# An mLSTM cell followed by a tanh-shrink MLP: ranks of a list schedule from due times, scores of the first two units ahead of their gates, shorter fillers, and a last output in four blocks

## The chip, the core and the metric

The kernel runs on one core of one Trainium2 chip. The metric is the device time of one execution, in microseconds (us), as the median of several runs. Below, PE is the TensorE engine, DVE is VectorE, ACT is ScalarE, POOL is GpSimd and SP is SyncE; PEld is PE's loading of weights, which overlaps its matmuls.

## The reference

Everything is float32. A recurrent cell with a matrix as its state runs over time for each batch and head; its output is reshaped to 3072 tokens of 320 features and goes through two matrix products with `h - tanh(h)` between them.

```python
batch, n_heads, seq, head_dim = (4, 8, 768, 40)
for t in range(S):
    m_new = np.maximum(f_gate[:, :, t] + m, i_gate[:, :, t])
    f_stab = np.exp(f_gate[:, :, t] + m - m_new)
    i_stab = np.exp(i_gate[:, :, t] - m_new)
    m = m_new
    C = f_stab[:, :, None, None] * C + i_stab[:, :, None, None] * np.einsum('bhd,bhe->bhde', vt, kt)
    n = f_stab[:, :, None] * n + i_stab[:, :, None] * kt
    h_tilde = np.einsum('bhde,bhe->bhd', C, qt)
    denom = np.maximum(np.abs(np.einsum('bhd,bhd->bh', n, qt)[:, :, None]), 1.0)
    y[:, :, t] = h_tilde / (1.0 + np.exp(-o_gate[:, :, t])) / denom
# bridge: (B,H,S,D) -> (B*S, H*D)
x = np.ascontiguousarray(y.transpose(0, 2, 1, 3)).reshape(B * S, H * D)
# MLP: n_tokens, d_model, d_ff = (3072, 320, 2048)
h = x @ w_in
g = h - np.tanh(h)
out = (g @ w_out).astype(np.float32)
```

## The kernel before

**Units of the cell.** The recurrence is done in chunks of 128 time steps, in closed form. A *unit* is one batch element with all 8 heads in one chunk: 4 batches x 6 chunks are 24 units, numbered chunk by chunk, so units 0 to 3 are the first chunk. For each unit the kernel makes the scores `ps` (PE, from the loaded `kz` and `qz`), a causal mask of them in `P` (DVE; for the units in `BY_POOL` ACT copies and POOL selects), the values scaled by gate factors in `vs` (DVE, with one more column from ACT), the sum over the chunk in `ph` (PE), the division by the denominator and the output gate (`den`, `o`, `ys`: DVE and ACT; the division by shares of heads on ACT is called "shares"), the update of the state (`pc` on PE, the decay of `state`), and the transposes of `ys` to `xT` (`px` on PE), which is the input of the MLP. Units of later chunks go through DRAM for the transpose (`zt` to `h_rows` to `z_in`, `yt` to `y_rows` to `xT`). The gate factors of a chunk are made from the loaded gates by two transposes and two products on PE (`gate`), with rows of DVE and ACT work between.

**The MLP.** Two units make a *group* of 256 tokens: 12 groups. The 2048 hidden features are 8 pairs of 128-feature blocks. An *item* is one group with one or a few pairs: `ph_up` (PE, h), the squares and polynomials of `g` (`z`, `q`, `gt` on ACT and DVE), and the product with `w_out` (`po`). Groups 0 and 1 run in plain form while the weights still arrive, in the nine items 0 to 8 of `RUNS`. From `START`, item 9, on, groups 2 to 11 use seven products in place of eight for each 2 x 2 block of blocks (products `ph_up<-xT,sums_in` and `pS`, with sums of weights `sums_in` and differences of weights `wT` made once, and sums `s` of `gt`). Here ACT carries partial sums from bank to bank (`ph_up<-ph_up`). This is the *long stage*.

**The weights** come in as pieces of a 64-bit format and are put together on the chip: POOL issues the fetch into a buffer `w`, ACT makes two parts (`w_e`, `w_r`), DVE shifts one, an adder makes `w_m`, and DVE sets the sign into `w_in` or `w_out`. The string `ADDERS` says for each of the 16 blocks whether the adder is POOL (G) or DVE (V). There are four buffers `w`; a fetch waits for the `sign` step of the block four earlier.

**What sets the order.** The program is written out by a list scheduler, the class `Plan` (L135). Each operation is added with an engine, a modelled duration, the operations that it needs, the buffers (tokens) that it takes and gives, and a rank. `run` (L214) picks, over and over, the ready operation with the earliest modelled start, and by rank where starts tie; an operation with a positive rank is charged `WAIT` = 0.2188 us of start. Its choice is then fixed: `Pinned` and `T.keep` chain each engine's instructions in that order, so on the chip an engine never overtakes its own queue. The table `BY` says which engine does which kind of step. `plan_gates`, `plan_unit`, `plan_weights`, `plan_plain`, `plan_down`, `plan_seven` and `plan_late` add the operations.

**Fillers.** Where the model sees PE idle before the long stage, `idle` and `stream` (L445) put in matmuls of a constant tile `lit` into a bank that nobody reads (`awake<-lit`, 128x512). They compute nothing. Their number is fixed when the program is written; the chip runs them whether PE would have waited or not.

**The end.** `last_parts` adds the last group's banks of products together into `ob` on DVE in three steps and stores each from SP; the register load `load_count` prepares a branch to a fallback that the runs here don't take.

Of the kernel before, what the change touches and what calls it, by code (L numbers as in the profile page):

```python
# [60 lines left out]
L = 128  # L61
# [18 lines left out]
def kernel(  # L80
# [54 lines left out]
    class Plan:  # L135
# [8 lines left out]
        AGE = -0.4021  # L144
# [10 lines left out]
        def add(self, engine, us, step, after=(), rank=0.0, take=(), give=(), at=0.0, kb=0.0, tiles=1, hold=0.0, dense=1.0, lag=None, small=False, port=False, late=False):  # L155
# [3 lines left out]
                  "lag": self.LAG[engine] if lag is None else lag, "small": small, "port": port and engine in "VG", "late": late}  # L159
# [53 lines left out]

        def run(self, idle, fill):  # L214
            for op in self.todo:
                op["then"] = []
# [151 lines left out]
    G.memset(k_tiles[:, :, H:], 0.0)  # L368
    G.memset(vs_tiles[:, :, H * D1:], 0.0)
# [35 lines left out]
    load_unit(0, ("qz",), A)  # L405
    load_gates(0, 1)
# [10 lines left out]
    load_unit(1, ("qz",), A)  # L417
# [18 lines left out]
    load_unit(0, ("v",), G)  # L436
# [546 lines left out]
    def down_seven(some):  # L983
# [4 lines left out]
        def product(where, a, x, b):  # L988
# [4 lines left out]
            if first:  # L993
                pool, tag = ((ps_o, "po0"), (ps_o, "po1"), third[g])[bank]
                tag = tag if isinstance(tag, str) else tag["small"]
                pS[g][bank] = pool.tile([128, 2 if bank else 3, HM], FP, name=f"pS{bank}", tag=tag)
# [5 lines left out]
        for k in (0, 1, 5, 3, 4, 2, 6) if final else range(7):  # L1002
            for x, (_, p) in enumerate(some):
# [3 lines left out]
                    ((0, 2), a11, even[:, 0]), ((0, 0), a12, odd[:, 0]), ((2, 1), a22, wT[p][:, 3]),  # L1007
# [34 lines left out]
    def last_parts(g):  # L1042
# [11 lines left out]
        def store(x, n=1):  # L1054
            at = [out[row_of(g * GT + y // 2):, y % 2 * HM:].offset for y in (x, x + n - 1)]
            blocks = [[at[1] - at[0], n]] if n > 1 else []
            SP.dma_start(out=bass.AP(out.tensor, at[0], [[DM, L], *blocks, [1, HM]]), in_=ob[:, x:x + n] if n > 1 else ob[:, x])

        def first():
            A.copy(out=a, in_=bank[0][:, 2])  # L1060
            V.tensor_tensor(out=ob[:, 0:5:4], in0=bank[0][:, 0:2], in1=twice(a), op=OP.add)
            store(0)

        def second():
            V.tensor_tensor(out=u, in0=bank[1], in1=twice(ob[:, 4]), op=OP.add)
            V.tensor_tensor(out=ob[:, 3], in0=bank[1][:, 0], in1=u[:, 1], op=OP.add)
            store(3)
# [251 lines left out]
    RANKS = (-1.0, -1.0, 15.2966, -19.6693)  # L1319
    WEIGHTS = (0.08, -3.8727, 8.9593, 4.7376, 13.1429, 47.5005, 2.7491, 9.7033)  # L1320
    START = item(FIRST * NP)
    LATER_GATES = (13.4508, 52.4651)
    SECOND_GATES = (7.6004, 15.8868)
    HOLD = 16.8771
    FETCH = {(0, 1): 6.5462, (2, 1): -9.4480, (3, 0): 9.5391, (3, 1): 34.7367}
    APART = ()
# [60 lines left out]
    LATE = {"o": -4.9124, "k": -11.0257, "q2": -0.0286, "v": 0.9346}  # L1387

    def plan_unit(n, rank):
# [10 lines left out]
        if n < 2:  # L1400
            u["qz"] = plan.add("N", 0.0, lambda: arrive(n), at=(6.4, 7.8)[n] - 1.7)
            if n == 0:
                u["v"] = plan.add("N", 0.0, lambda: None, at=7.0 - 1.7)
            else:
                u["v"] = plan.add("G", 0.6, lambda: [load_unit(n, ("v",), G), arrive(n)], at=5.5, rank=-1.0, kb=164)
# [10 lines left out]
        def first_part():  # L1416
# [4 lines left out]
            for step in ready[0]:  # L1421
# [594 lines left out]
```

## Time and profile before

| what | value |
|---|---|
| three runs, us | 511.04, 505.89, 509.83 |
| median, us | 509.83 |
| profiled execution, us | 506.61 |
| its span, us | 504.9 |
| mean granted PE clock | 0.996 |
| bytes moved | 52.39 MB, 104 GB/s over the span |
| first product in seven (start of the long stage) | 127.72 us |
| last matmul ends | 498.08 us |

The span runs from the first to the last instruction of the profiled execution; its own time also holds what lies around the span, 1.7 us. All instants and durations of the trace belong to that execution, which is 3.2 us shorter than the median of the three runs.

### The profile page before, as it was taken

What the parts mean: (1) busy time and instruction counts of PE and PEld (TensorE: products, weight loads), DVE (VectorE), ACT (ScalarE), POOL (GpSimd) and SP (SyncE); (2) the same over time, 40 slices, a digit from 0 to 9 for tenths busy, and PEclk for the clock granted to TensorE, in tenths of its full rate; (3) what the DMA queues carried; (4) which work ended last, traced back from release to release, by engine and by line L of the source; (5) the groups of instructions that cost most, each with busy time, mean ns of one, the idle gap of its engine ahead of it and who ended that gap; (6) DMA issues with size and microseconds to landing.
All of it is one profiled execution on the core that took longest, in us unless ns stands there. A gap on an engine that the chain in (4) does not pass through costs nothing.

```text
span 504.9 us, 14174 instructions
## 1 busy us (share of the span) xinstructions
PE 494.6 (98%) x5376; PEld 433.5 (86%) x5376; DVE 381.9 (76%) x928; ACT 298.4 (59%) x832; POOL 174.7 (35%) x294
## 2 busy tenths in 40 slices
PE   8999999999999999999999999999999999999994
PEld 4775776777799999999999999999999999899984
DVE  3779989656578778788788788788788788685853
ACT  3465675365467567557567567557567666654540
POOL 4698987686542143041243043042022020000000
PEclk9999999999999999999999999999999999999998
DMA  7964675353543643542643553553443452310001
GB/s 225 285 207 128 205 190 147 61 99 88 117 100 81 127 101 77 112 110 68 132 110 84 109 113 87 107 111 85 93 103 86 89 107 44 71 31 0 27 1 32
DMA packets 138217, 52.39 MB, mean 104 GB/s; under 512 B 116512, under 2 KB 129504, under 8 KB 138144
## 3 DMA queue, kind: packets, MB, share of 16 engines
q1 hardware_dynamic: 126888, 27.50, 26.9%
q0 software_dynamic: 8032, 20.00, 14.2%
q10 hardware_dynamic: 3224, 3.93, 2.3%
q8 instruction: 44, 0.72, 0.6%
q14 instruction: 29, 0.24, 0.2%
HBM read 38.94 MB, written 12.45 MB: 102 GB/s over the span
## 4 chain that ended last, share of the span: by engine, by line
PE 89%; DVE 6%; issue 2%; POOL 1%; ACT 0%; DMA 0%; SPq 0%; DVEq 0%; ACTq 0%
PE ph_up L129 38%; PE pS L129 30%; PE po L129 6%; PE pT L129 5%; PE ps L129 3%; PE awake L129 3%; DVE gt L106 2%; PE pc L129 2%; POOL w_m L106 1%; PE ph L129 1%; DVE w_e L106 1%; DVE sums_in L106 0%; DMA z_in<-h_rows 0%; PE gate L129 0%; DVE w_out L106 0%
## 5 line engine op out<-in xcount | busy, mean ns | idle before, releaser
L129 PE MATMUL ph_up<-xT,w_in 64*64 64x256 f32 (+3 forms) x1316 | 156.5, 349 | 0.0
L129 PEld LDWEIGHTS ph_up<-xT,w_in 128*128 128x128 f32 (+2 forms) x1316 | 114.6, 162 | 18.5 <-issue 5.2
L106 POOL TENSOR_TENSOR ys<-z_in,o 128x256 f32<-128x256 f32 (+1 forms) x40 | 22.9, 583 | 239.2 <-ACT o L106 229.3
L129 PE MATMUL ph_up<-xT,sums_in 128*128 128x128 f32 x624 | 95.5, 276 | 0.7 <-issue 0.5
L106 ACT ACTIVATE z<-ph_up 128x256 f32<-128x256 f32 (+1 forms) x98 | 40.7, 417 | 87.5 <-PE ph_up L129 87.2
L129 PEld LDWEIGHTS ph_up<-xT,sums_in 128*128 128x128 f32 x624 | 84.9, 191 | 2.4 <-ACT ph_up L106 0.8
L129 PE MATMUL pS<-wT,s 128*128 128x160 f32 x480 | 81.4, 300 | 0.0
L106 DVE TENSOR_TENSOR both<-ph_up,cs 128x256 f32<-128x256 f32 x78 | 32.9, 422 | 62.7 <-PE ph_up L129 60.2
L106 DVE SCALAR_TENSOR_TENSOR gt<-q,gt 128x512 f32<-128x512 f32 (+1 forms) x98 | 71.3, 735 | 7.4 <-ACT q L106 1.0
L106 ACT COPY ph_up<-ph_up 128x256 f32<-128x256 f32 x117 | 41.8, 357 | 57.5 <-PE ph_up L129 48.8
L106 ACT ACTIVATE q<-z,tiny 128x512 f32<-128x512 f32 (+1 forms) x98 | 69.9, 713 | 1.9
L129 PEld LDWEIGHTS pS<-wT,s 128*128 128x128 f32 x480 | 69.0, 190 | 0.4 <-issue 0.4
L106 ACT ACTIVATE o<-o,den 128x40 f32<-128x40 f32 x168 | 56.4, 411 | 5.9 <-DVE den L106 5.9
L129 PE MATMUL pS<-w_out,gt 128*128 128x160 f32 x320 | 56.6, 311 | 0.0
L129 PEld LDWEIGHTS pS<-w_out,gt 128*128 128x128 f32 x320 | 45.1, 190 | 4.4 <-issue 2.3
L106 DVE SCALAR_TENSOR_TENSOR gt<-ph_up,z 128x256 f32<-128x256 f32 (+1 forms) x98 | 41.4, 457 | 6.0 <-ACT z L106 6.0
L106 POOL DMA_DIRECT2D v<-in_v x62 | 37.5, 609 | 2.0 <-issue 2.0
L129 PE MATMUL po<-w_out,gt 128*128 128x320 f32 x128 | 37.7, 440 | 0.2 <-DVE gt L106 0.2
L129 PEld LDWEIGHTS po<-w_out,gt 128*128 128x128 f32 x128 | 23.3, 190 | 9.6 <-DVE gt L106 0.9
L106 DVE TENSOR_TENSOR s<-gt 128x256 f32<-128x256 f32 x80 | 30.6, 405 | 0.3
L129 PE MATMUL pS<-wT,gt 128*128 128x160 f32 x160 | 29.9, 300 | 0.0
L129 PE MATMUL pS<-w_out,s 128*128 128x160 f32 x160 | 28.9, 300 | 0.1
(122 smaller groups left out, 728.0 us busy)
## 6 DMA issues: line engine op xcount, KB each, us to landing
w<-in_moe_w_out POOLq DMA_DIRECT2D x8, 640.0 KB, 5.1
h_rows<-zt SPq DMA_DIRECT2D x80, 64.0 KB
z_in<-h_rows SPq DMA_DIRECT2D x80, 64.0 KB
w<-in_moe_w_in POOLq DMA_DIRECT2D x16, 256.0 KB, 4.1
kz<-in_kT SPq DMA_DIRECT2D x48, 80.0 KB
qz<-in_qT SPq DMA_DIRECT2D x44, 80.0 KB
o<-in_o_gate POOLq DMA_DIRECT2D x20, 160.0 KB, 2.6
y_rows<-yt SPq DMA_DIRECT2D x80, 40.0 KB
```

The lines of the kernel that those rows point to most:

```text
L106: i = method(*args, **kwargs)
L129: return cls.keep(nc.tensor.matmul(*args, **kwargs))
```

## The change

The work stays the same but for the fillers; what moves is where each instruction stands in its engine's queue, and for some which engine it is on.

1. *Ranks from due times.* Operations of the long run of items get a due time (`due`), and a pass backward through the plan hands it to what they need, less durations. Off PE an operation's rank is now this due time plus `BLEND` = 0.1443 of its old rank. About forty rank constants have new values.
2. *Scores first.* For units 0 and 1 the scores are issued in two halves ahead of the gates' PE work; unit 1's go into the two banks of `ph_up` (`APART`). The loads of unit 1's `qz` (ACT's queue) and unit 0's `v` (POOL's queue) move to the head, two memsets on POOL behind them.
3. *Other engines.* `ADDERS` has another pattern, the decay of `state` goes from DVE to POOL, and the differences `wT` that are made late from POOL to DVE.
4. *Fillers* can be a quarter to a whole of 512 columns long, and `idle` counts them in quarters up to 14 us.
5. *The last output* is made and stored in four blocks in place of three, the last one in two halves of 64 rows from SP and ACT; `load_count` comes behind it.

```diff
+        BLEND = 0.1443
         def run(self, idle, fill):
+            for op in reversed(self.todo):
+                for a in op["after"]:
+                    a["due"] = min(a["due"], op["due"] - a["us"] - (0.0 if a["engine"] == op["engine"] == "T" else a["lag"]))
+            for op in self.todo:
+                if op["engine"] != "T":
+                    op["rank"] = op["due"] + self.BLEND * op["rank"]
...
-    ADDERS = "GGGGGVGGGGVGVGVV"
+    ADDERS = "VGGGVVGGGGVGVGVV"
-    BY = {"prep": "V", "share": "A", "product": "G", "decay": "V", "sum_in": "G", "sum_out": "V", "late_out": "G", "kz": "S", "qz": "S", "v": "G", "k": "G", "o": "G", "out": "S", "in": "S", "y": "S", "x": "S"}
+    BY = {"prep": "V", "share": "A", "product": "G", "decay": "G", "sum_in": "G", "sum_out": "V", "late_out": "V", "kz": "S", "qz": "S", "v": "G", "k": "G", "o": "G", "out": "S", "in": "S", "y": "S", "x": "S"}
...
     load_unit(0, ("qz",), A)
+    load_unit(1, ("qz",), A)
+    load_unit(0, ("v",), G)
     load_gates(0, 1)
...
     def stream(bank, n):
-        for _ in range(n):
-            T.matmul(bank.rearrange("p (h t) -> p h t", h=HH), lit, lit.unsqueeze(1).to_broadcast([128, HH, L]), start=True, stop=True)
+        for first in range(0, n, HH):
+            k = min(HH, n - first)
+            T.matmul(bank.rearrange("p (h t) -> p h t", h=HH)[:, 0:k], lit, lit.unsqueeze(1).to_broadcast([128, k, L]), start=True, stop=True)
...
         def first():
             A.copy(out=a, in_=bank[0][:, 2])
             V.tensor_tensor(out=ob[:, 0:5:4], in0=bank[0][:, 0:2], in1=twice(a), op=OP.add)
-            store(0)
+            store(0, SP)
...
         def third():
-            V.tensor_tensor(out=ob[:, 1:3], in0=bank[2], in1=u, op=OP.add)
-            store(1, 2)
-        in_parts.extend((second, first, third))
+            V.tensor_tensor(out=ob[:, 2], in0=bank[3][:, 0], in1=u[:, 1], op=OP.add)
+            store(2, A)
+        def fourth():
+            V.tensor_tensor(out=ob[:, 1], in0=bank[2][:, 0], in1=u[:, 0], op=OP.add)
+            store(1, SP, A)
+        in_parts.extend((first, second, third, fourth))
...
-    RANKS = (-1.0, -1.0, 15.2966, -19.6693)
+    RANKS = (-1.0, -1.0, 18.2675, -24.8287)
-    APART = ()
+    APART = (1,)
...
+        if n < 2:
+            names = ("up0", "up1") if n in APART else ("a",)
+            op = plan.add("T", 0.5, first_part, [u["qz"]], rank, [(name, held) for name in (*names, "P")], tiles=2, dense=0.6)
+            u["scores"] = plan.add("T", 0.5, other_part, [op], rank, tiles=2, dense=0.6)
...
+    DUE0, DUE1 = 19.0, 4.7354
+    def when(x):
+        return DUE0 + DUE1 * (sum(map(len, items[:x])) + 2 * max(0, x - len(items)))
...
-            if final and k == 5 and ends:
-                downs.append(plan.add("T", 0.1, load_count, [op], rank))
+            if final and k == 6 and ends:
+                downs.append(plan.add("T", 0.1, load_count, [op, e], rank))
...
-        one = 0.43 if t0 < plan.COLD[0] else 0.217
+        one = 0.108 if t0 < WARM else 0.217
```

Three places in the queues follow. Each row is an instruction or a run of equal ones (x8), with its line, its operation, the tile that it writes and the tiles that it reads.

The first place is PE's queue at the start of the program: the scores `ps` of units 0 and 1, the gates' transposes and products `gate`, and the fillers `awake` around them. Before, the scores of unit 0 stand behind the gates:

```order
L129 LDWEIGHTS lit
L129 MATMUL awake<-lit 128x512
L133 MATMUL gate<-ident,sums_in 128x32
L133 MATMUL gate<-ident,xT_90 128x32
L129 MATMUL gate<-lfT,upto 128x32
L129 MATMUL gate<-lfT,ones 120x32
L129 MATMUL ps<-qz,kz 128x128 x8
L129 LDWEIGHTS lit
L129 MATMUL awake<-lit 128x512
```

And now:

```order
L129 LDWEIGHTS lit
L129 MATMUL awake<-lit 128x128
L129 MATMUL ps<-qz,kz 128x128 x16
L133 MATMUL gate<-ident,sums_in 128x32
L133 MATMUL gate<-ident,xT_90 128x32
L129 LDWEIGHTS lit
L129 MATMUL awake<-lit 128x512
L129 MATMUL gate<-lfT,upto 128x32
L129 MATMUL gate<-lfT,ones 120x32
```

Both units' scores (x16) have moved ahead of the gates' first transpose, and one filler stands between the transposes and the products. Ahead of these rows stood 9 full fillers before and stand 7 and a quarter now.

The second place is PE's queue around the `ph` of the first chunk's last units, with items of the MLP (`ph_up`, `po`) between. Before:

```order
L129 MATMUL ph<-vs,P 128x41 x8
L129 MATMUL ph_up<-xT_87,w_in 128x256 x2
L129 MATMUL ps<-qz,kz 64x2x64 x4
L129 MATMUL ps<-qz,kz 64x64 x4
L129 MATMUL ps<-qz,kz 64x2x64 x4
L129 MATMUL ps<-qz,kz 64x64 x4
L129 MATMUL gate<-ei,ident 64x32 x2
L129 MATMUL po<-w_out,gt 128x320 x4
L133 MATMUL px<-ident,ys_144 128x128 x3
```

Behind these rows 25 full fillers follow, and then the `ph` of unit 3. Now:

```order
L129 MATMUL ph_up<-xT_87,w_in 128x256 x2
L129 MATMUL ph<-vs,P 128x41 x8
L129 MATMUL ph_up<-xT_87,w_in 128x256 x4
L129 MATMUL po<-w_out,gt 128x320 x2
L133 MATMUL px<-ident,ys_146 128x128 x3
L129 MATMUL pc<-vs,k 64x41 x8
L129 MATMUL po<-w_out,gt 128x320 x2
L133 MATMUL px<-ident,ys_145 128x128 x3
L133 MATMUL gate<-ident,sums_in 128x32
```

Between the two `ph` of the last units now stand two fillers and two products of `ph_up`, and no run of fillers is left at this place.

The third place is POOL's queue at about the fourth block of weights: the fetches of blocks (`DMA`), the adds `w_m`, and the two selects of unit 2's masks in `P`. Before:

```order
L106 DMA w_345<-in_moe_w_in 128x256 x2
L106 DMA w_345<-in_moe_w_in 64x128 x2
L106 TENSOR_TENSOR w_m<-w_e,w_r 128x640
L106 AFFINE_SELECT P<-P 128x512
L106 TENSOR_TENSOR w_m<-w_e,w_r 128x640
L106 AFFINE_SELECT P<-P 128x512
```

And now:

```order
L106 DMA w_319<-in_moe_w_in 128x256 x2
L106 DMA w_319<-in_moe_w_in 64x128 x2
L106 TENSOR_TENSOR w_m<-w_e,w_r 128x640
L106 TENSOR_TENSOR sums_in<-w_in 128x2x128
L106 TENSOR_TENSOR sums_in<-w_in,sums_in 128x128
L106 DMA w_388<-in_moe_w_out 128x2x320
L106 TENSOR_TENSOR w_m<-w_e,w_r 128x640
L106 AFFINE_SELECT P<-P 128x512 x2
```

The two selects stood apart behind one add each; now both stand behind two adds, two sums and another fetch. Over the whole program the count of full fillers on PE goes from 94 to 29, with 5 of half and 1 of a quarter length beside them; POOL's adds go from 11 to 9 and DVE's from 5 to 7; 32 differences `wT` move from POOL to DVE and 16 decays from DVE to POOL.

More of the change, by code (lines that the diff above doesn't have):

```diff
@@ L153, in __init__, with add @@
             self.port = {"V": 0.0, "G": 0.0}
-        def add(self, engine, us, step, after=(), rank=0.0, take=(), give=(), at=0.0, kb=0.0, tiles=1, hold=0.0, dense=1.0, lag=None, small=False, port=False, late=False):
+        def add(self, engine, us, step, after=(), rank=0.0, take=(), give=(), at=0.0, kb=0.0, tiles=1, hold=0.0, dense=1.0, lag=None, small=False, port=False, late=False, due=1000.0):
             self.serial += 1
@@ L1052, in twice, with store @@
             return t.unsqueeze(1).to_broadcast([128, 2, HM])
[L1054 to L1057, printed above, removed]
+        def store(x, *queues):
+            at = out[row_of(g * GT + x // 2):, x % 2 * HM:].offset
+            rows = L // len(queues)
+            for i, queue in enumerate(queues):
+                queue.dma_start(out=bass.AP(out.tensor, at + i * rows * DM, [[DM, rows], [1, HM]]), in_=ob[i * rows:(i + 1) * rows, x])
         def first():
@@ L1425, in plan_unit @@
         bank = "a"
-        u["scores"] = plan.add("T", 1.0, first_part, [u["qz"], *(of(n - 2, "second") if n in (2, 3) else [])], rank, [(bank, held), ("P", held)], tiles=2, hold=HOLD * (n // B), dense=0.4 if n else 0.6)
-        if n in BY_POOL:
+        if n < 2:
+            names = ("up0", "up1") if n in APART else ("a",)
+            op = plan.add("T", 0.5, first_part, [u["qz"]], rank, [(name, held) for name in (*names, "P")], tiles=2, dense=0.6)
+            u["scores"] = plan.add("T", 0.5, other_part, [op], rank, tiles=2, dense=0.6)
+            u["mask"] = [plan.add("V", 0.62, lambda i=i: ready[1][i](), [u["scores"]], rank - 7.2169, give=[(names[i], held)] if n in APART else [(names[0], held)] if i else ())
+                         for i in range(2)]
+        else:
+            u["scores"] = plan.add("T", 1.0, first_part, [u["qz"], *(of(n - 2, "second") if n in (2, 3) else [])], rank, [(bank, held), ("P", held)], tiles=2, hold=HOLD * (n // B), dense=0.4 if n else 0.6)
+        if n < 2:
+            pass
+        elif n in BY_POOL:
             copies = [plan.add("A", 0.55, lambda i=i: ready[1][i][0](), [u["scores"]], rank - -2.0678, give=[(bank, held)] if i else ()) for i in range(2)]
@@ L1430, in plan_unit @@
         else:
-            u["mask"] = [plan.add("V", 0.62, lambda i=i: ready[1][i](), [u["scores"]], rank - 10.5159, give=[(bank, held)] if i else ())
+            u["mask"] = [plan.add("V", 0.62, lambda i=i: ready[1][i](), [u["scores"]], rank - 6.0391, give=[(bank, held)] if i else ())
                          for i in range(2)]
@@ L1453, in plan_unit @@
             steps = []
-            over = plan.add("V", 0.6, lambda: [steps.extend(gate(n, in_parts=True)), steps[0]()], [op], rank - 2.4035)
+            over = plan.add("V", 0.6, lambda: [steps.extend(gate(n, in_parts=True)), steps[0]()], [op], rank - -0.7648)
             shares = plan.add("A", 1.9, lambda: steps[1](), [over, u["open"]], rank + -2.2635)
-            u["gate"] = plan.add("V", 0.5, lambda: steps[2](), [shares, *of(n - 2, "turn")], rank - 3.2112, give=[("small", held)])
+            u["gate"] = plan.add("V", 0.5, lambda: steps[2](), [shares, *of(n - 2, "turn")], rank - -4.8960, give=[("small", held)])
         else:
@@ L1680, in plan_seven @@
         again1 = shrink_op("A", 0.62, "again1", [square], -3.1099)
+        for later in (second, copy_d, copy_e):
+            later["due"] = when(x) + 1.5
         cube_b = shrink_op("V", 0.41, "cube_b", [add_e], -14.4883, [("up1", held_1)])
@@ L1807, in idle @@
                 n = 0
-        return n * one
+        return n * (0.108 if t0 < WARM else 0.217 / HH)
     plan.run(idle, lambda t0, t1: idle(t0, max(t1, t0 + 0.25), 1.0))
```

85 lines of the change are left out of this document (44 added, 41 removed).

## The prediction

> **What bounds the kernel now.** I read the page first, then TensorE by stretches, then the chain of waits and the timeline of the first 130 us. The page's head and the shares of its chain (section 4) say whose kernel this is:
>
> ```profile
> span 504.9 us, 14174 instructions
> PE 494.6 (98%) x5376; PEld 433.5 (86%) x5376; DVE 381.9 (76%) x928; ACT 298.4 (59%) x832; POOL 174.7 (35%) x294
> PE 89%; DVE 6%; issue 2%; POOL 1%; ACT 0%; DMA 0%; SPq 0%; DVEq 0%; ACTq 0%
> ```
>
> TensorE (PE) is busy for 98% of the span. Its idle time is no reserve, so the question is what it does while it is "busy". Two stretches (time, then busy time and count by engine, clock, DMA), and the groups of instructions of the first 128 us for one tile:
>
> ```profile
> 0.00:127.70 127.70, 125.09 (x1018) 88.76 (x1019) 96.00 (x204) 68.84 (x164) 97.40 (x156) 1.00 0.60 164
> 127.70:498.10 370.40, 369.53 (x4359) 344.77 (x4357) 285.45 (x724) 229.54 (x668) 77.31 (x139) 1.00 0.39 84
> L129 PE MATMUL awake<-lit 128*128 128x512 bf16 x94 | 26.3, 428 | 1.1 <-DVE probe L106 1.1
> ```
>
> The second stretch, from the first item in seven products to the last matmul, has under 1 us of idle PE in 370, and its matmuls are the reference's own work. The first holds 94 matmuls on `lit`, which compute nothing: they fill time in which PE would wait. So 26 us of the first 128 are **waiting dressed as work**; that is what a new order can win. PE's open waits there are 127.7 - 125.1 - 1.1 (the start) = 1.5 us.
>
> What are the fillers waiting for? The timeline of the dearest place, PE's rows, then DVE's and ACT's:
>
> ```profile
> 39.10 5.56 PE L129 MATMUL awake<-lit 128*128 128x512 bf16 x25
> 44.50 1.87 PE L129 MATMUL ph<-vs,P 128*128 128x41 f32 x16
> 42.23 0.48 DVE L106 TENSOR_TENSOR vs<-v,ei 128x320 f32<-128x320 f32 x1
> 43.79 0.20 ACT L106 ACTIVATE vs<-ei 128x8 f32<-128x8 f32 x1
> ```
>
> PE idles in disguise until the fourth unit's scaled values `vs` are there; DVE makes them at 42.2 and ACT adds their column at 43.8. Nothing but a place in DVE's queue holds them up. The bound is PE in the long stage, and in the first stage the order of DVE's and POOL's queues.
>
> **The change, term by term.** I work against the profiled execution's own time, 506.61 us (span 504.9, and 1.7 around it). It lies 3.2 us under the median shown, 509.83.
>
> *Fillers removed.* The order counts 94 full fillers before and, of pieces, 31.75 full lengths after. Pieces of the chain price them, with the scores' and `ph` rows that are wanted below:
>
> ```profile
> 1.13 4.02 PE awake L129 x9
> 6.78 2.01 PE ps L129 x16
> 8.79 3.96 PE awake L129 x9
> 12.74 1.36 PE ps L129 x16
> 15.98 1.71 PE ph L129 x16
> 58.27 2.91 PE awake L129 x13
> ```
>
> Cold, one takes 4.02 / 9 or 3.96 / 9 = 0.443; later 2.91 / 13 = 0.224. Before: 18 x 0.443 + 76 x 0.224 = 25.0 us (the 26.3 above counts modelled ends that overlap). After: 7.25 ahead of the scores, 1 among the gates' products and 6.5 behind them stand in the cold part, 17 later: 14.75 x 0.443 + 17 x 0.224 = 10.3. **-14.7 us**, if nothing takes the fillers' place. The rest of PE's work up to the long stage is the same list of matmuls.
>
> *Scores of units 0 and 1 first.* Unit 1's products move into the cold part: 2.01 instead of 1.36, **+0.65**. A new wait stands at the head of the queue: PE reaches unit 0's scores at 1.13 + 7.25 x 0.443 = 4.3 and unit 1's at 6.3, and behind them wait the gates' transposes, on which every `vs` hangs. When does their data land?
>
> ```profile
> 1.73 1.54 SPq L106 DMA_DIRECT2D kz<-in_kT  x4
> 3.38 0.84 SPq L106 DMA_DIRECT2D o<-in_o_gate  x2
> 7.78 0.47 ACT L106 ACTIVATE o<-o 128x320 f32<-128x320 f32 x1 [0.34 <-DMA o<-in_o_gate]
> ```
>
> The nearest transfer with an end, `o`, is issued from 3.38 and lands at 7.8, 4.4 us. Unit 1's `kz` is issued at about 2.5 to 3.3, so at worst it lands near 7.3, 1 us late; unit 0's scores began at 6.78 without a wait, so theirs is 0 to 2.5 us late. I take **+1.0**, range 0 to 2.5. [...]
>
> *Unit 2's masks on POOL.* They stand behind more POOL work than before. The prices, and the DVE rows that set the start:
>
> ```profile
> L106 POOL DMA_DIRECT2D w<-in_moe_w_in x32 | 18.0, 568 | 12.7 <-DVE w_in L106 5.8 <-ACT vs L106 5.4 <-DVE sums_in L106 1.5
> L106 POOL TENSOR_TENSOR w_m<-w_e,w_r 128x640 int32<-128x640 int32 x11 | 17.5, 1594 | 7.7 <-DVE w_e L106 7.6
> L106 POOL TENSOR_TENSOR sums_in<-w_in 128x256 f32<-128x256 f32 x8 | 6.7, 842 | 1.3 <-DVE w_in L106 1.3
> L106 POOL TENSOR_TENSOR sums_in<-w_in,sums_in 128x128 f32<-128x128 f32 x16 | 8.3, 528 | 0.2
> L106 POOL DMA_DIRECT2D w<-in_moe_w_out x8 | 5.9, 738 | 1.4 <-ACT w_e L106 1.3
> L106 POOL TENSOR_SCALAR_AFFINE_SELECT P<-P 128x512 f32<-128x512 f32 x2 | 1.5, 758 | 0.0
> 16.84 0.16 DVE L106 SCALAR_TENSOR_TENSOR den<-inv,ph 128x8 f32<-128x8 f32 x1 [0.61 <-PE ph L129]
> 19.41 0.16 DVE L106 SCALAR_TENSOR_TENSOR den<-inv,ph 128x8 f32<-128x8 f32 x1 [0.39 <-PE ph L129]
> 21.30 0.82 DVE L106 SCALAR_TENSOR_TENSOR w_in<-w,w_m 128x640 int32<-128x640 int32 x1
> ```
>
> Before, the first block of weights was done at 22.1, behind both units' gates on DVE. After, it stands ahead of unit 1's gate (19.41 to 21.30, 1.9 us less), and unit 0's starts 2.2 earlier: its `ph` ends on PE at 1.1 (start) + 6.5 (14.75 cold fillers) + 4.0 (two cold scores) + 1.3 (the gates' products: 6.78 - 5.15 less their waits of 0.3) + 1.7 (`ph`) = 14.6, against DVE's 16.84 behind it. 22.1 - 1.9 - 2.2 = 18.0. Then POOL fetches a block (4 x 0.57), adds one (1.59), makes two sums (0.84 + 0.53), fetches (0.74), adds (1.59) and selects (0.76): 8.3 us, so unit 2's first mask is there at 26.3. PE gets to its `ph` at 14.6 + 1.7 (unit 1's `ph`) + 9 warm fillers (2.0) + the scores of units 2 and 3 (2.2, somewhat under 1.36 each) + item 0's six products (2.6, half of them full) + transposes and `pc` (about 1.2) = 24.3. The wait ahead of the scores moves both alike. **+2.0**, range 0 to 3.5.
>
> *DVE's and POOL's shares.* In the first stage DVE gains two blocks' adds and some of the 32 differences of `w_out`, and loses the decays:
>
> ```profile
> L106 DVE CUSTOM_DVE_ANT_0 w_m<-w_e,w_r 128x1280 uint16<-128x1280 uint16 x5 | 4.9, 991 | 0.0
> L106 DVE TENSOR_TENSOR xT<-xT 128x128 f32<-128x128 f32 x20 | 4.8, 282 | 0.0
> L106 DVE TENSOR_TENSOR s<-gt 128x256 f32<-128x256 f32 x80 | 30.6, 405 | 0.3
> L106 DVE TENSOR_TENSOR state<-state,eN 120x164 f32<-120x164 f32 x16 | 5.7, 354 | 0.1
> L106 POOL TENSOR_TENSOR wT<-w_out 128x160 f32<-128x160 f32 x13 | 7.3, 562 | 0.0
> ```
>
> A difference of 128x160 is not shown on DVE: between 0.28 (128x128) and 0.41 (128x256), near the first, 0.32. Up to the long stage: 2 x 0.99 + 10 x 0.32 - 3 x 0.35 = +4.1 on 96.0, in some 115 us in place of 127.7. DVE goes from 75% to 87%. The other 22 differences (7 us) meet 13 decays less (4.6) in the long stage, where DVE is at 77% and PE hides it: nothing. A decay on POOL, 0.5 to 0.6 by `wT`'s row, is hidden by that engine's 80% of idle time there. A fuller DVE makes PE wait somewhere: I take **+0.7**, half of the 1.5 of open waits once more, and up to 6. The old open waits, 1.5, go in good part: **-1.0**.
>
> *The end.*
>
> ```profile
> 496.78 2.62 SPq L106 DMA_DIRECT2D out<-ob  x3
> 497.55 0.33 DVE L106 TENSOR_TENSOR ob<-pS,u 128x160 f32<-128x160 f32 x1
> 498.20 0.49 DVE L106 TENSOR_TENSOR ob<-pS,u 128x320 f32<-128x320 f32 x1 [0.32 <-PE pS L129]
> 500.00:501.00 1.00, 0.00 (x0) 0.00 (x0) 0.00 (x0) 0.00 (x0) 0.00 (x0) 1.00 0.56 160
> ```
>
> The chain of DVE's last steps loses a register load (0.2) and has 0.33 + 0.33 for 0.49: about 0.1 earlier. The last issue ran from 498.7 to 499.4; halves on two queues cost about half that, 0.35, and half the bytes save about 0.25 of the last microsecond. **-0.7**, range -1.2 to 0 (the register loads now stand behind the store). [...]
>
> **Sum:** -14.7 + 0.65 + 1.0 + 2.0 + 0.7 - 1.0 - 0.7 = -12.05, so 494.6 in the profiled execution's terms, 497.8 beside the median. The long stage starts at 127.7 - 11.35 = 116.4, all but the end's term counted.
>
> **Rivals.** *The clock stays low.* The clock column reads 1.00 from the start, yet the rows show fillers at 0.443 up to 12.7 and half that later. The first full stretch, 4.02 us, did not lift the rate, the second, 3.96, did. After, the full stretches are 3.2 and 2.9 us. If the rate then rises only with item 0's matmuls, 9 fillers (2.0), two scores (2 x 0.9), transposes and six products (about 2.5) lose 6.3; some 2 of it hides in the waits that I have counted: +4, 501.8. [...] *DVE becomes the bound.* Its share over a fuller stretch before:
>
> ```profile
> 20.00:90.00 70.00, 68.79 (x573) 48.53 (x572) 62.19 (x116) 44.06 (x105) 60.01 (x82) 1.00 0.62 180
> ```
>
> It kept 62.19 of 70 us, 89%, there, and 75% over the whole first stage. The forecast asks for 100.1 of 116.4, 86%, over the whole. If it keeps 82%, the long stage begins at 100.1 / 0.82 = 122.1, 5.7 later: 503.5. Against it: the 89% lasted for 70 us. *Slower:* in the long stage ACT carries PE's partial sums from bank to bank, and the new order puts a pair of shares between two copies:
>
> ```profile
> 269.78 0.36 ACT L106 COPY ph_up<-ph_up 128x256 f32<-128x256 f32 x1 [0.67 <-PE ph_up L129]
> 270.05 1.35 ACT L106 ACTIVATE o<-o,den 128x40 f32<-128x40 f32 x4
> ```
>
> ACT was idle for 0.67 ahead of that copy, and two shares take 0.68: they just fit. If they don't, PE stalls; at 0.68 for each of 39 items it is 26 us, and the time 524 (497.8 + 26). It decides from 0.45 us an item. Against it: six products of `pS`, 0.8 us, still stand in between.
>
> **Chances.** Forecast 0.60, clock 0.18, DVE 0.15, slower 0.07. All new waits at nothing and the end at its best give 493 beside the median, 490 by itself; the new waits at their upper ends (2.5, 3.5, 6), nothing saved elsewhere, 507. So 490 to 506. A change under 1% (below 504.7 or above 514.9) can't be told from none: faster 0.80, same 0.14, slower 0.06.
>
> **What would show it.** Fillers of about 10 us and the first product in seven near 116: the main term. A wait of PE at unit 2's `ph` for POOL: the masks. Fillers at 0.44 behind the first `ph`: the clock. DVE above 90% before 116 with PE waiting for `gt` or `vs`: the second rival. PE waiting for ACT's `ph_up` behind 120: the slower one. I am wrong altogether if fillers are gone and PE's open waits have grown by as much.

## The result, and the profile after

The changed kernel takes 504.92 us in the median of 20 runs (499.98 to 509.10), the kernel before 509.86 (505.18 to 513.14). The ratio is 0.9893, with a 95% interval of 0.9862 to 0.9924. Here and below a median or a range takes in all runs, while a ratio and its interval leave out runs that lie more than 1.5% above the fastest of their kernel, so the two can differ. So 5 us were won where 12 were forecast. The profiled execution took 503.09 us with a span of 501.4, against 506.61 and 504.9 before.

The page's head and the shares of its chain, after:

```profile
span 501.4 us, 14062 instructions
PE 486.4 (97%) x5317; PEld 430.8 (86%) x5317; DVE 387.1 (77%) x947; ACT 295.1 (59%) x832; POOL 168.6 (34%) x276
PE 83%; DVE 8%; DMA 2%; issue 2%; ACT 2%; POOL 1%; SPq 1%; DVEq 0%; POOLq 0%; ACTq 0%
```

The chain leans less on TensorE (83% for 89%) and more on VectorE and DMA. Then the stretches: everything up to the long stage, which starts at 125.80 us (127.72 before), and below it the fillers alone (time, busy time and count of TensorE; after the other engines follow clock, DMA share, GB/s):

```profile
0.00:125.80 125.80, 117.55 (x959) 86.52 (x960) 101.69 (x211) 67.09 (x164) 87.25 (x135) 0.93 0.62 167
0.00:600.00 600.00, 11.06 (x35) 0.98 0.37 87
```

The fillers are gone as counted: 11.1 us of them are left of 26.3. But the long stage comes only 1.9 us sooner. TensorE now stands idle for 8.2 us of that stage (125.80 - 117.55) where it stood 2.6, its mean granted clock is 0.93, and VectorE is busy for 101.7 us where it was 96.0. The waits of TensorE in that stage, and the clock (column before the DMA share) in three waits, each followed by the stretch behind it:

```profile
PE ph_up L129 <- DVE gt L106: 3.0, 2, 1.7
PE ps L129 <- DMA kz<-in_kT: 2.2, 2, 1.8
PE gate L133 <- DVE state L106: 1.9, 1, 1.9
29.10:30.80 1.70, 0.02 (x1) 0.00 (x0) 1.70 (x4) 0.47 (x2) 0.24 (x1) 1.00 0.33 136
31.50:38.50 7.00, 7.00 (x28) 5.41 (x27) 4.78 (x11) 3.96 (x11) 6.98 (x12) 0.51 0.48 142
62.50:64.30 1.80, 0.00 (x0) 0.00 (x0) 1.80 (x5) 0.43 (x1) 1.80 (x4) 1.00 0.00 0
65.10:69.00 3.90, 3.90 (x12) 3.00 (x13) 3.89 (x9) 2.45 (x5) 3.88 (x4) 0.58 0.16 35
99.90:101.10 1.20, 0.00 (x0) 0.00 (x0) 1.20 (x3) 1.20 (x4) 1.18 (x3) 1.00 0.76 311
101.20:110.00 8.80, 8.80 (x92) 6.71 (x96) 7.05 (x15) 2.60 (x7) 6.06 (x11) 1.00 0.44 93
```

In each of the three waits TensorE is idle and VectorE is busy for the whole of it. Behind the first two the clock is at about half for 7 and 4 us; behind the third it is not. By these shares some 5.1 us are lost, 0.49 x 7.0 + 0.42 x 3.9. What VectorE did ahead of the first wait, and GpSimd beside it (start, duration):

```profile
25.87 3.83 DVE L106 TENSOR_TENSOR vs<-v,ei 128x320 f32<-128x320 f32 x2
26.61 1.57 POOL L106 TENSOR_TENSOR w_m<-w_e,w_r 128x640 int32<-128x640 int32 x1
28.11 1.23 POOL L106 TENSOR_SCALAR_AFFINE_SELECT P<-P 128x512 f32<-128x512 f32 x2
L106 DVE TENSOR_TENSOR vs<-v,ei x24: 447/486/3425, 13.5 to 407.4; 128x320 f32<-128x320 f32 x24
L106 DVE SCALAR_TENSOR_TENSOR gt<-ph_up,z x18: 405/675/692, 30.4 to 121.7; 128x512 f32<-128x512 f32 x14, 128x256 f32<-128x256 f32 x4
```

The last two rows give the shortest, the median and the longest of one. Two `vs` normally take 1.0 us; here one of them took 3.43, 2.9 us over the median, and it ended when GpSimd's add and both selects were through (29.70 against 29.34). `gt<-ph_up,z`, which reads one operand from PSUM, stayed between 0.41 and 0.69 us. So by these rows a VectorE instruction can stand for 2.9 us while GpSimd works beside it; which of the two waits for the other they don't show, since this `vs` began 0.3 us ahead of the add (26.28 and 26.61). Instructions with one operand were longer too, such as the copy shown with the first run below (2.18 us in place of 0.2) and the shift `w_e` in the next rows (1.83 in place of 0.44).

Ahead of the second wait, the one for the gates, VectorE stands in the same way. The shift `w_e` takes 0.44 us at its shortest, and this operation on `xT` took 0.67 in the kernel before:

```profile
58.51 1.83 DVE L106 TENSOR_SCALAR w_e<-w_e 128x640 int32<-128x640 int32 x1
60.86 2.01 DVE L106 TENSOR_TENSOR xT<-xT,xT 32x512 f32<-32x512 f32 x1
58.12 1.87 POOL L106 TENSOR_TENSOR w_m<-w_e,w_r 128x640 int32<-128x640 int32 x1 [0.49 <-DVE w_e L106]
60.48 1.85 POOL L106 TENSOR_TENSOR w_m<-w_e,w_r 128x640 int32<-128x640 int32 x1 [0.49 <-ACT q L106]
DVE w_out L106 <- POOL w_m L106: 1.1, 1, 1.1
```

The last row is from VectorE's waits in this stage. Its open waits for a `w_m` of GpSimd come to only 1.1 us (4.0 before), so an add that merely comes late is not what holds it up. So there were three candidates for the missing 7 us: the clock, VectorE's own work, and GpSimd standing in VectorE's way.

### The profile page after: what moved, and what is told of

It is laid out like the page before. It is cut to its first block, busy times and chain, and to the rows that moved or that the text cites. A ratio compares the mean times of both kernels' runs of the same rounds, so it can differ in the third digit from the quotient of the medians.

```text
span 501.4 us, 14062 instructions
## 1 busy us (share of the span) xinstructions
PE 486.4 (97%) x5317; PEld 430.8 (86%) x5317; DVE 387.1 (77%) x947; ACT 295.1 (59%) x832; POOL 168.6 (34%) x276
## 4 chain that ended last, share of the span: by engine, by line
PE 83%; DVE 8%; DMA 2%; issue 2%; ACT 2%; POOL 1%; SPq 1%; DVEq 0%; POOLq 0%; ACTq 0%
PE ph_up L129 37%; PE pS L129 30%; PE po L129 4%; PE pT L129 4%; PE ps L129 3%; PE pc L129 2%; DVE vs L106 1%; DVE gt L106 1%; PE ph L129 1%; DMA o<-in_o_gate 1%; DMA kz<-in_kT 1%; DVE xT L106 1%; DVE w_e L106 1%; DVE den L106 1%; PE awake L129 1%
## 5 line engine op out<-in xcount | busy, mean ns | idle before, releaser
L129 PE MATMUL ph_up<-xT,w_in 64*64 64x256 f32 (+3 forms) x1316 | 160.2, 352 | 3.5 <-DVE gt L106 3.0
L129 PEld LDWEIGHTS ph_up<-xT,w_in 128*128 128x128 f32 (+2 forms) x1316 | 115.8, 164 | 24.5 <-issue 7.8
L129 PE MATMUL pS<-wT,s 128*128 128x160 f32 x480 | 79.3, 301 | 0.0
L106 DVE SCALAR_TENSOR_TENSOR gt<-q,gt 128x512 f32<-128x512 f32 (+1 forms) x98 | 64.5, 673 | 2.6 <-ACT q L106 0.6
L129 PE MATMUL pS<-w_out,gt 128*128 128x160 f32 x320 | 57.8, 311 | 0.0
L129 PE MATMUL po<-w_out,gt 128*128 128x320 f32 x128 | 39.4, 449 | 0.0
```

The costliest lines, as they stand in the source:

```text
L106: i = method(*args, **kwargs)
L129: return cls.keep(nc.tensor.matmul(*args, **kwargs))
```

## Experiments

**The clock: 17 fillers more.** In a hook ahead of TensorE's operations 22 and 69 of the plan:

```diff
+                    more(self.count_t)   # 8 fillers into bank a0 at 22, 9 into po1 at 69
                     n = idle(self.free["T"], t)
```

> The changed kernel with 17 more fillers and nothing else: eight full ones where its TensorE stood idle from 29.1 to 30.8 us, nine where it stood idle from 62.5 to 64.4. At 0.217 us each they fit into the two waits. Theory A (the fillers also kept the clock up; two open waits of 1.7 and 1.9 us let it fall to half for 6.9 and 3.9 us): the granted clock stays at 1.00 from 15 us on, the work behind each place is 3.4 and 1.9 us sooner, the long stage starts near 120.5 instead of 125.8, and the time is about 499.5 against 504.9, ratio to the kernel before about 0.979. Theory B (a filler is only a wait in disguise, the rows at half rate have another cause): the clock dips stay, the time stays within 0.5 us of 504.9, ratio 0.989 to 0.991. Theory C (VectorE is the bound): the clock stays up, but TensorE then waits longer for gt or vs further on, and less than 2 us are won, ratio 0.985 to 0.989.

Measured: 505.46 us, ratio 0.994 (0.9905 to 0.9976); the long stage at 125.26. Its stretches around the two places:

```profile
30.00:45.00 15.00, 13.34 (x112) 9.97 (x111) 13.15 (x34) 9.67 (x26) 12.13 (x18) 1.00 0.48 136
60.00:75.00 15.00, 13.07 (x108) 9.08 (x106) 14.19 (x27) 7.50 (x19) 14.97 (x19) 1.00 0.38 109
PE gate L133 <- DVE state L106: 1.9, 1, 1.9
PE px L133 <- DVE ys L106: 1.6, 1, 1.6
38.70 0.52 PE L133 MATMUL px<-ident,ys 128*128 128x128 f32 x3 [1.60 <-DVE ys L106]
35.98 2.18 DVE L106 COPY ys<-ys 128x64 f32<-128x64 f32 x1
```

The clock stayed at 1.00, as theory A had it, and nothing was won: TensorE came sooner and waited longer, for `ys` (a copy that took 2.18 us in place of 0.2) and for the gates. Theory A falls as the cause; theory C, or another cause on VectorE, is left.

**The same from the other side: 25 fillers fewer before.**

```diff
+            if n and pool and 35.0 < t0 < 41.6:
+                pass
-            if n and pool:
+            elif n and pool:
```

> The kernel before without the 25 fillers at 39.1 to 44.5 us, nothing else changed. What follows them waits for vs in any case, so nothing starts later for lack of data. Theory A: TensorE is idle for some 5 us, its clock falls to half for 4 to 7 us behind that, and the time is 2 to 3.5 us above the kernel before (ratio 1.004 to 1.007). Theory B: the wait is open instead of filled, the time is the same (ratio 1.000 within 0.002).

Measured: 508.86 us, ratio 0.9991 (0.9952 to 1.0029). In its profile TensorE waits 3.9 us for `vs`, and its clock falls to 0.65 behind that:

```profile
36.80:40.70 3.90, 0.00 (x0) 0.02 (x1) 3.90 (x8) 3.90 (x12) 3.88 (x7) 1.00 0.58 194
40.70:45.00 4.30, 4.29 (x21) 3.24 (x21) 4.30 (x3) 0.81 (x3) 4.29 (x6) 0.65 0.48 152
```

The dip came, the loss of time did not show: the interval reaches from a gain of 2.4 us to a loss of 1.5. The first step of the prediction, that these fillers are waiting in disguise, holds.

**Masks and one add on VectorE.**

```diff
-        masks = [(lambda i=i: copy(i), lambda i=i: select(i)) if n in BY_POOL ...
+        masks = [(lambda i=i: mask(i), lambda: None) if n in BY_POOL ...
+        adders = ADDERS[:2] + "V" + ADDERS[3:]
```

> The changed kernel with the two selects of unit 2's masks and the add of the third block of weights done by VectorE at the places where ScalarE's copies and GpSimd's add stood; VectorE gains 2 x 0.62 + 0.88 = 2.1 us of work there. Theory D (the vs that took 3.43 us from 26.3 was held up by the three GpSimd operations beside it): every vs takes about 0.5, gt comes at 29.5 to 30.2 instead of 30.35, and the wait of TensorE of 1.7 us becomes 0.8 to 1.6; if it falls under the 1.3 us that another wait of the same run had without a dip, the clock stays at 1.00 there and the time is 1.5 to 4 us below 504.9. Rival (the vs is slow by itself, its operands late): it stays at 3.4 and the added work comes on top, so the time is 2 us above 504.9.

Measured: 503.85 us, ratio 0.9875 (0.9818 to 0.9931), not told apart from the changed kernel. At the place itself each `vs` takes 0.48, as theory D had it; another one, further on, takes 3.2, again beside an add:

```profile
L106 DVE TENSOR_TENSOR vs<-v,ei x24: 442/484/3221, 13.2 to 412.1; 128x320 f32<-128x320 f32 x24
102.72 3.22 DVE L106 TENSOR_TENSOR vs<-v,ei 128x320 f32<-128x320 f32 x1
104.03 1.55 POOL L106 TENSOR_TENSOR w_m<-w_e,w_r 128x640 int32<-128x640 int32 x1
```

It ended 0.36 us behind GpSimd's add (105.94 and 105.58), just as the one at the first place ended 0.36 behind the selects (29.70 and 29.34). By its row it began 1.3 us ahead of that add, when GpSimd was issuing DMAs, so the rows don't show what it stood for at first. One place mended, the next one stands: inconclusive for the time.

**Gates ahead of the scores again.**

```diff
-            u["qz"] = plan.add("N", 0.0, lambda: arrive(n), at=(4.3, 5.1)[n] - 1.7)
+            u["qz"] = plan.add("N", 0.0, lambda: arrive(n), at=(6.2, 7.0)[n] - 1.7)
```

> The changed kernel with one number changed: the scheduler's model has the scores' data of units 0 and 1 land at 6.2 and 7.0 us, as the trace shows, instead of 4.3 and 5.1. It then places the gates' work of TensorE ahead of the scores, as in the kernel before, and everything behind that is planned anew, with 60.5 full lengths of fillers in place of 31.75. Theory E (scores first costs: a wait of 2.2 us, and the gates 5 us later): unit 0's first ph starts at 11 to 12.5 instead of 14.8, no wait on kz, and with no clock dip from the denser fillers the long stage starts at 121 to 124, time 500 to 503. Rival (the order at the start is worth little, the fillers that the new plan adds take the gain): long stage at 125 to 127, time 504 to 506.

Measured: 508.10 us, ratio 0.9984 (0.9950 to 1.0018). Unit 0's `ph` starts at 11.34 for 14.80, as theory E had it, but the long stage at 130.55. The new plan differs in too many places to say what the order at the start is worth; that stays open.

**Six fillers more at the start**, by the same hook:

```diff
+                    more(self.count_t)   # 6 fillers at operation 0, the first scores
```

> The changed kernel with six more full fillers at the start and nothing else: the first stretch of fillers, 7.25 lengths from 1.13 to 4.40 us, then a wait for kz to 6.19 and 7.03, becomes 13.25 lengths to about 7.0, so the wait is filled and little is added (at most 0.8 us). In five profiled executions the first matmuls at full rate came at 4.9 (with nine fillers ahead, the kernel before less 25), 12.7 (the kernel before), 14.5 and 14.3 (the changed kernel and the one with 17 more fillers) and near 29 and 25 (the other two): the same instructions at the start, another time of the rise. Theory F (the rise needs an unbroken dense stretch, and with stretches of 3.3 and 2.7 us it is a matter of chance, which makes the changed kernel's slower executions of 507 to 509 us): the rise comes at or before 8 us in most executions, the scores take 1.2 instead of 2 us each, unit 0's ph starts at 11.5 to 13 instead of 14.8, fewer executions lie above 506, the median is 501 to 503, ratio 0.982 to 0.987. Rival (the stretch does not matter, the added fillers only delay): first rise as scattered as before, median 505 to 506, ratio 0.990 to 0.993.

Measured: 503.92 us, ratio 0.9884 (0.9846 to 0.9921). The nine executions lie between 501.95 and 505.01, none above 506 where the changed kernel had 8 of 20. In the profiled one the scores took 1.55 and 1.44 us for 16 each (2.08 at half rate in the kernel before, 1.16 at full rate in the run without 25 fillers), but the clock is back at 0.55 between 15 and 30 us. The spread shrank as theory F had it, the median did not move by more than its uncertainty. (The changed kernel's spread is that of 20 executions.)

**No shifts on VectorE.**

```diff
-            e = plan.add("V", 0.47, shift, [e], r, port=True)
+            e = plan.add("V", 0.47, lambda: None, [e], r, port=True)
```

> The changed kernel without VectorE's 16 shifts w_e of the weights' conversion, 11.2 us of its 102.8 us before the long stage (the weights come out wrong; all else as it was, the same order of everything else and the same fillers). Theory C (from 15 us on VectorE's queue is the bound, and TensorE's open waits and dips of the clock come from it): the waits for gt and for the gates' transposes shrink below 1 us, no dip of the clock in the middle, and the long stage starts 4 to 7 us sooner, near 120; time 498 to 501, ratio 0.977 to 0.982. Theory A alone (TensorE's rate bounds, VectorE has slack): under 1.5 us sooner, time 503 to 505, ratio 0.987 to 0.990.

Measured: 500.79 us, ratio 0.9842 (0.9788 to 0.9896); the long stage at 123.08. Between the two theories: 11.2 us of work taken away give 2.7 in the profile and 4.1 in the median.

**The end alone**, on the kernel before: the diff's part on the last output and nothing else.

> The kernel before with the changed last output only: four blocks, the last in halves from SyncE and ScalarE, the register loads behind it. The span from the start of the last four matmuls (497.37 before, 495.16 after) to its end was 7.53 us in the kernel before and 6.24 in the changed one. If the end is worth what the difference of the two says, 1.29, this kernel shows 6.1 to 6.4; if it is worth the 0.7 that was forecast, 6.8; a rival is that the difference comes from elsewhere and it stays at 7.5.

```profile
497.95 0.71 PE L129 MATMUL pS<-w_out,s 128*128 128x160 f32 x4
498.14 0.89 DVE L106 TENSOR_TENSOR ob<-pS,u 128x160 f32<-128x160 f32 x3
498.49 1.32 SPq L106 DMA_DIRECT2D out<-ob  x2
498.72 1.02 ACTq L106 DMA_DIRECT2D out<-ob  x2
```

With a span of 504.2 that is 6.25 us, against 7.53 before and 6.24 after: the end is worth 1.3 us.

**No adds on GpSimd.** VectorE's shift writes `w_m` itself where GpSimd was the adder; what is left out are the lowest three bits of these weights, less than the expectation says.

```diff
         def shift():
-            V.tensor_single_scalar(w["e"], w["e"], 3, op=OP.logical_shift_left)
+            V.tensor_single_scalar(w["m" if adder == "G" else "e"], w["e"], 3, op=OP.logical_shift_left)
         def whole():
+            if adder == "G":
+                return
```

> The changed kernel without GpSimd's nine adds w_m, some 14.5 us of its 87.3 us before the long stage (VectorE's shift writes w_m itself, so the weights come out wrong; the order of all else and the fillers stay). The run without VectorE's shifts moved the start of the long stage by 2.7 us for 11.2 us of work taken from VectorE. Theory G (GpSimd's queue, busy 14.5 of 15 us between 60 and 75 in that stage, is what VectorE and through it TensorE wait for, and its operations stretch VectorE's beside them): the stretched vs of 3.4 us goes below 2.2, the waits of TensorE for gt and the gates shrink, the long stage starts 3 to 6 us sooner than 125.8, time 499 to 502, ratio 0.979 to 0.985. Theory C (VectorE's own work is the bound): less than 1.5 us sooner, time 503.5 to 505, ratio 0.988 to 0.990.

Measured: 498.90 us, ratio 0.9715 (0.9668 to 0.9762).

```profile
0.00:123.29 123.29, 119.89 (x959) 88.74 (x960) 90.72 (x211) 66.73 (x164) 70.95 (x126) 0.90 0.62 170
L106 DVE TENSOR_TENSOR vs<-v,ei x24: 444/485/748, 13.2 to 404.4; 128x320 f32<-128x320 f32 x24
```

The same 211 instructions of VectorE take 90.7 us in place of 101.7: 11.0 us of its busy time had been standing, 5.9 of it on the eight `vs` of that stage (9.5 us with the adds, 3.6 without). The longest `vs` is 0.75. No wait of TensorE for VectorE is left in that stage. TensorE was at half rate until 31 us in this execution, so the start of its long stage is not compared.

**Neither shifts nor adds of GpSimd.** For GpSimd's nine blocks ScalarE's second part is written to `w_m` itself, and VectorE's shift is left out everywhere.

> The changed kernel without VectorE's shifts and without GpSimd's adds (ScalarE writes w_m itself; the weights come out wrong): 11.2 us less on VectorE and 14.5 less on GpSimd, TensorE's work and fillers as in the changed kernel. If the two queues together hold TensorE back, its open waits before the long stage go from 7.1 to below 4 and the clock dips in the middle go: the long stage starts at 116 to 120, where the forecast had it (116.4), time 495 to 498, ratio 0.971 to 0.977. If what is left is the start (kz, the gates behind the scores, the late rise of the clock), the long stage starts at 120 to 123, time 498 to 501, ratio 0.977 to 0.983.

Measured: 492.92 us, ratio 0.9681 (0.9639 to 0.9723).

```profile
0.00:115.13 115.13, 111.78 (x959) 82.54 (x960) 85.28 (x195) 66.84 (x164) 69.92 (x126) 0.97 0.66 182
PE ps L129 <- DMA kz<-in_kT: 2.1, 2, 1.5
```

The long stage starts at 115.1; the forecast had 116.4. The only open wait left ahead of it, after the start, is the one for `kz`. With VectorE free, TensorE's list of matmuls takes the time that the prediction gave it.

**The two edits that came out lowest one by one, together**: the masks and one add on VectorE, and six fillers at the start.

> The changed kernel with the six fillers more at the start and with the masks of unit 2 and the third block's add on VectorE, the two edits that came out lowest one by one (503.92 and 503.85 us against 504.92). If their gains add up: 502.5 to 503.5, ratio 0.984 to 0.987, and no execution above 506. If both are chance: 504 to 505, ratio 0.988 to 0.990.

Measured: 506.08 us, ratio 0.9910 (0.9883 to 0.9936). The gains did not add; nothing shows that either was more than chance.

**The same adds taken from the kernel before**, by the same edit.

> The kernel before without GpSimd's eleven adds w_m (VectorE's shift writes w_m itself, so the lowest three bits of these blocks of weights are left out); order and fillers as before. In the changed kernel the same edit took 6 us off the time and 11.0 us off VectorE's busy time before the long stage (101.7 to 90.7) with the same 211 instructions. Theory H (before, the 94 fillers set TensorE's pace and GpSimd's adds hid behind them; the changed kernel took the fillers away and met the adds): at most 2 us faster than the kernel before, ratio 0.996 to 1.000, though VectorE's busy time falls from 96.0 to about 86. Rival (the adds cost the same in both kernels, so they explain nothing of the difference): 5 to 7 us faster, ratio 0.986 to 0.990.

Measured: 505.50 us, ratio 0.9944 (0.9906 to 0.9982).

```profile
0.00:127.08 127.08, 124.36 (x1019) 89.14 (x1020) 87.90 (x204) 68.77 (x164) 79.99 (x145) 0.97 0.59 165
```

VectorE loses 8.1 us of busy time here too (96.0 to 87.9), but the kernel moves by only 2.9 us (0.9 to 4.8), a little more than theory H allowed. (The long stage starts 0.6 us sooner, but this execution ran at about half rate from about 21.8 to 28.7 us, with a mean clock of 0.77 from 15 to 30 us, and the kernel before did not, so the two starts are not comparable.) In the changed kernel the same edit gave 0.9715 against 0.9893, 1.8% or 9 us (6 by the medians). So part of the price, about a third, was paid before as well; the rest came in with the change. That the fillers had hidden it is the likely reason, not a shown one.

**Shift and add as one instruction of VectorE.** A carry out of the lowest three bits is left out.

```diff
         def whole():
-            ENGINES[adder].tensor_tensor(out=w["m"], in0=w["e"], in1=w["r"], op=OP.add)
+            V.scalar_tensor_tensor(out=w["m"], in0=w["e"], scalar=3, in1=w["r"], op0=OP.logical_shift_left, op1=OP.bitwise_or)
```

> The changed kernel with shift and add of every block of weights as one VectorE instruction, a shift and a bitwise or of 128x640 (0.8 us by the row of the sign step of the same size), in place of VectorE's shift (16) and of the adds on GpSimd (9) and VectorE (7); a carry out of the lowest three bits is left out. VectorE: 16 x 0.8 for 11.2 + 6.2, so 4.6 us less, and the stretch of 11 us by GpSimd's adds gone; GpSimd 14.5 less. If the adds on GpSimd are what held the first stage, it comes out with or below the run without them: 495 to 499, ratio 0.969 to 0.978, the long stage from 116 to 123 by when the clock rises. If the order of VectorE's queue is what counts: 502 to 504.

Measured: 498.64 us, ratio 0.9798 (0.9746 to 0.9851); the long stage at 117.88, VectorE busy for 91.4 until there.

**The same with eleven fillers more at the start**, by the hook: six at operation 0, five at operation 8, unit 0's first `ph`.

> The same fused kernel with six more full fillers ahead of the first scores (into the wait for kz) and five behind the gates' products (2.2 us at half rate, 1.1 at full). In the runs without GpSimd's adds the executions fell in two groups, 493 and 498 to 501, and the profiled one of the second group had TensorE at half rate until 30 us. Theory F (the second group is the late rise of the clock, and dense fillers make the early rise likelier): the second group gets rarer, the spread of the executions shrinks to below 5 us, the median is 1 to 3 us below that of the fused kernel. Rival (the added fillers are only in the way): 0.5 to 2 us above it.

Measured: 496.95 us, ratio 0.9770 (0.9732 to 0.9808); six executions from 496.46 to 499.33 where the kernel without them had 495.29 to 501.49.

**All adds on VectorE, the arithmetic unchanged.**

```diff
-            ENGINES[adder].tensor_tensor(out=w["m"], in0=w["e"], in1=w["r"], op=OP.add)
+            V.tensor_tensor(out=w["m"], in0=w["e"], in1=w["r"], op=OP.add)
```

> The changed kernel with all 16 adds w_m on VectorE, nine of them moved there from GpSimd at the same places of the order; the arithmetic is the changed kernel's. VectorE gets nine instructions of 0.83 us more, 7.5 us. Theory G (while GpSimd runs an add, VectorE's instructions with two operands beside it stand; that stretch was 11.0 us): VectorE's busy time before the long stage goes from 101.7 down to about 98 although its work grows, the long stage starts 2 to 5 us sooner than 125.8, time 499 to 503, ratio 0.978 to 0.986. Theory C (VectorE's own work is the bound): its busy time goes to 109, the long stage starts 2 to 3 us later, time 507 to 508, ratio 0.994 to 0.997.

Measured: 497.55 us, ratio 0.9788 (0.9735 to 0.9841). The profiled execution is again one with TensorE at half rate until 30 us, so its long stage, at 127.7, says nothing; VectorE's row does:

```profile
0.00:127.70 127.70, 122.26 (x960) 89.80 (x961) 98.97 (x219) 66.74 (x164) 71.94 (x126) 0.99 0.60 164
```

VectorE does nine adds more and is busy for 2.7 us less. Theory G foretold 98; theory C 109. Which instructions stand was not tested: theory G names those with two operands, and the shift `w_e` that took 1.83 us beside an add has one. With the arithmetic unchanged, this version is faster than both kernels: its interval lies below the changed kernel's, 0.9862 to 0.9924.

**The same with the eleven fillers.**

> The same with the eleven fillers more at the start that the fused kernel had in the run before (six into the wait for kz, five behind the gates' products). There the spread of six executions went from 6.2 to 2.9 us and the median 1.7 us down. Theory F: here too the executions above the median by over 3 us disappear and the median lies 1 to 2 us below the kernel without them. Rival: no difference, or 1 us above.

Measured: 497.77 us, ratio 0.9790 (0.9745 to 0.9835).

```profile
0.00:119.84 119.84, 114.19 (x971) 82.54 (x971) 97.42 (x219) 67.15 (x164) 70.58 (x126) 0.99 0.63 175
```

One execution of six (501.18) lies over 3 us above the median, where the kernel without them had two (503.03 and 504.56); the median is the same. With an early rise of the clock the long stage comes at 119.8. So theory F is borne out for the spread, which shrank three times of three, though here one execution of the kind that was to go is left; for the median it is borne out once. Four profiles caught a late rise, at 25 to 31 us (masks on VectorE, gates first, no adds on GpSimd, all adds on VectorE), and in three of them the execution is among the longer ones of its kernel (not with the gates first). No kernel was profiled in both groups, so that these are the late rises is likely, not shown.

## Why the prediction was wrong in size

**The step that failed is the price of a fuller VectorE**: "A fuller DVE makes PE wait somewhere: I take **+0.7**". The busy time behind it came out near, 100.1 us forecast and 101.7 measured; what failed is that VectorE would fit it in beside TensorE. In place of +0.7 the profile has 4.9 us of TensorE's open waits for VectorE (3.0 for `gt`, 1.9 for the gates) and some 5.1 us lost at half rate behind them, and the long stage starts 9.4 us later than the 116.4 that was forecast. The reason is that the durations were taken from rows as if they were VectorE's work. Of the 96.0 us before, 8.1 were standing that goes when GpSimd's adds go; in the changed kernel 11.0 of 101.7 were. The profile before had signs of it that the prediction does not speak of: a mean of 547 ns for `vs` up to the long stage, with 482 as usual, and one `gt<-q,gt` of 4.03 us. It had to be asked what VectorE could do at most when the fillers no longer hid it.

The price in the end: with the adds away from GpSimd the ratio is 0.9788 in place of 0.9893, 5.4 us (7.4 by the medians, 497.55 against 504.92). The forecast, 497.8 of 509.83, is a ratio of 0.9764, so 6.6 us were missing, and this is most of them, not shown to be all. The rival "DVE becomes the bound" had the right place, a share of 82% against a measured 101.7 / 125.8 = 81%, and 503.5 us; its reason was wrong, since with more work but less standing VectorE bound less.

**Fillers removed**: -14.7 forecast, 15.2 by the busy rows (26.3 to 11.1). Right. That they were waiting in disguise is borne out by the run without 25 of them; that nothing would take their place was the condition, and it was not met.

**Scores of units 0 and 1 first**: the cold scores of unit 1 cost 0.85 (all `ps` 23.86 us, 23.01 before) for +0.65. The wait for their data cost 2.2 for +1.0, inside its range of 0 to 2.5.

**Unit 2's masks on POOL**: +2.0 forecast, and TensorE never waited for them. The selects cost something else: they were two of the three instructions beside which the longest `vs` stood. The engine was right, the way was not.

**Old open waits** -1.0 and the new ones: all open waits after the first microsecond are 7.1 us, 1.5 before: the old ones went, and 4.9 for VectorE and 2.2 for `kz` came.

**The end**: -0.7 forecast, -1.3 measured, by one execution of the end alone and by the changed kernel's profile. By the prediction's own figures its 0.1 for VectorE's steps is 0.03 (0.2 + 0.49 - 0.66). What part the halves, the register loads behind the store and the shorter last step have in it was not measured apart; that halves cost about half of the issue, 0.35, and save 0.25 of the last microsecond was the author's estimate.

**The clock**: the rival had the rate stay low behind the first fillers, worth 4 us. The profiled execution after rose at 14.5 us, so the rival did not happen there; it did in three other profiles with the scores first (masks on VectorE, no adds on GpSimd, all adds on VectorE), which did not rise until about 30. The dips in the middle, 5.1 us, were not foreseen, but the run with 17 fillers more, without them, was no faster (0.994 against 0.9893): while VectorE was late anyway they cost nothing that shows.

**The slower rival**, ACT's shares in the long stage: TensorE waited 1.2 us for ACT's `ph_up` there in three places, not 26. It did not happen.

## What to carry to other kernels

Busy time of VectorE was not all work here (11.0 of 101.7 us went with GpSimd's adds): compare the shortest and the longest of one instruction in one row, and where they differ look at what GpSimd ran in that time. When a change takes away padding, ask first which engine sets the pace without it, and what that engine would need if nothing stood in its way. An operation put on a slower engine "because it is free" (an add took 1.57 us on GpSimd and 0.83 on VectorE) may cost more on the engine that it spares: here nine adds on GpSimd cost VectorE 11.0 us to save it 7.5.

## What the runs showed of the hardware

Full rate of TensorE came at about 5 us in three profiles and at 12.7 us in a fourth, nearly 8 us apart, though the instructions up to there were the same (the kernel before's start: the runs without 25 fillers, with the new end and without GpSimd's adds, and the kernel before itself).

In the changed kernel the clock fell to half after idle times of 1.70 and 1.90 us, for 7 and 4 us, and after one of 1.34 it did not. No limit follows from that. In the run with 17 fillers more, idle times of 1.60 and 1.93 passed without a dip; in the kernel before without GpSimd's adds it fell after idle times of 1.01 and 0.26; and in the run with six fillers more it fell at 14.9 us, for nearly 14 us, with no idle time above 0.39 in the 6 us ahead of it.

The clock's record shows 1.00 up to the first recorded change even where the matmuls run at half rate (fillers at 0.44 us up to 12.7 us in the kernel before, with 1.00 beside them), so at the start the durations are to be read, not the column.

Busy time of VectorE in the profile can be standing: the same 211 instructions were busy for 101.7 us beside nine adds of GpSimd and for 90.7 without them.
